# A new order of pieces in a fused attention and feed-forward kernel: chunk 0 projected block by block, logits in one group of eighty matmuls, softmax subtraction in place

## The chip, the cores and the metric

The kernel runs on one core of a Trainium2 chip. The metric is device time in microseconds (us) of one execution; three runs of the kernel before gave 234.38, 235.88 and 237.16 us, so its median is 235.88 us. Five engines work side by side: TensorE (PE in the profile; its weight loads are PEld), VectorE (DVE), ScalarE (ACT), GpSimd (POOL) and SyncE (SP), which here only issues DMAs. Each engine runs its own instructions strictly in the order in which the program lists them, and waits at one when an input or a buffer isn't ready.

## The reference

x is 2048 x 640 in bfloat16. The reference normalises it and adds two branches to it:

```python
xn = _layernorm(x, axis=-1)
return x + _A_ref(xn, A_wqkv, A_wo) + _B_ref(xn, B_w1, B_b1, B_w2, B_b2)

# A: attention of each position to 8 positions, 2 apart, back from itself; 32 heads of 20
qkv = (x @ wqkv) ...                       # 640 -> 3 * 640
idx = pos[:, None] - (jnp.arange(8) * 2)[None, :]
logits = jnp.einsum("bhsd,bhswd->bhsw", q, kg) * scale      # masked where idx < 0
o = jnp.einsum("bhsw,bhswd->bhsd", _softmax(logits), vg)
return o @ wo
# B: feed-forward, 640 -> 1536 -> 640
h = _gelu(x @ w1 + b1)
return h @ w2 + b2
```

## The kernel before, in words

The 2048 rows are cut in four chunks of 512 (CH), and each chunk in four blocks of 128. Channels lie on partitions in five tiles of 128 (KT). For each chunk n the work is:

- **Normalise and turn.** bn_stats on DVE (`do_st`, L437, two halves a block), sqrt on ACT (L458), reciprocal on DVE (L462). In chunk 0, DVE writes the normalised block (L478), PE turns it by five transposes (`do_tp`, L493) into PSUM, and ACT or DVE copies it to xnT (`do_tc`, L498). In chunks 1 to 3, ACT writes the normalised block xn (L474) and a DMA transpose on SP's queue turns it (`do_td`, L505). xn has two buffers, so ACT's third block of a chunk waits until the first block's DMA transpose has landed.
- **Projections.** q, k, v = xnT x wqkv. In chunks 1 to 3: fifteen pieces `pj` of five 128x512 matmuls (L537), each copied from PSUM by ACT (`pc`, L596). In chunk 0 before: q of blocks 0 and 1 in 128-column pieces (L550), everything else for pairs of blocks in 256-column pieces (L581).
- **Logits.** DVE multiplies q with k at each of the 8 offsets (`qk`, L611, eight instructions). PE sums over a head with twenty matmuls for each pair of offsets (L633). `do_max` (L646) and `do_sub` (L653) on DVE, exp on ACT (L663), sums, reciprocal and division on DVE (L669 to L681). DMAs spread the result over the 20 channels of a head (`ax<-attn`, L691: half on SP's queue, half on ACT's).
- **Values.** DVE multiplies v with ax (`av`, L707, eight), adds (L716, three) and writes oT (`ot`, L722).
- **Feed-forward.** PE: twelve pieces `f1` a chunk (L729, five 128x512 matmuls each); ACT: gelu (L740).
- **Output.** For each block five pieces `o`: four over the feed-forward's h, the fifth over oT (L760 for 512 columns, L762 for the other 128, seventeen pairs of matmuls in all). ACT copies it (L767, L768) and POOL adds it to the output with an accumulating DMA (L773). Before that, x is copied to the output by a plain DMA on SP's queue (`xp`, L514), and the bias b2 is added by an accumulating DMA that POOL issues (`xb`, L518) once that copy has landed.

Matmul results of the projections, `f1` and chunk 0 share four PSUM buffers ("acc"). The products `qk` and `av` share four SBUF buffers ("prod"). The logits have one PSUM tile.

**What sets the order.** `make_plan` (L149) lists all pieces with an engine, an estimated duration, a rank, the pieces they need and their buffers. `Plan.run` (L57) lays them out in time by these estimates: on each engine the ready piece with the lowest rank goes next. The program is emitted in that order. The table `RANK` shifts the rank of whole groups of pieces. So a changed rank, estimate or due time reorders the instructions of PE, DVE, ACT and SP, and nothing reorders them on the chip.

**Names used below**: `pj`, `f1`, `o`, `lg` (logits matmuls), `qk`, `av`, `ot`, `xn` and `tc` as above, then the chunk, then block or piece; `xd` and `xs` are the spreading DMAs on SP and ACT, `ld` is the loading of w2, wo and b2.

**In the emitted order of before** SP issues, after the first loads: the four transposes of chunk 1, `ld`, the four copies `xp0` to `xp3`, `xd0`, the eight transposes of chunks 2 and 3, `xd1` to `xd3`. POOL issues `xb0` to `xb3` as the copies land. PE has, around the middle of the span: eight `f1` of chunk 1, then the `pj` of chunk 2. ACT has, between the copies of chunk 1's and chunk 0's projections and the first gelu of chunk 1: `xn22` and `xn23`.

Of the kernel before, what the change touches and what calls it, by code (L numbers as in the profile page):

```python
# [10 lines left out]
ACT = mybir.ActivationFunctionType  # L11
# [7 lines left out]
class Plan:  # L19
# [112 lines left out]
RD = float(D) ** -0.5  # L132
# [3 lines left out]
WARM = 40  # L136

COLS = ((0, 2), (2, 4), (4, 5))
# [4 lines left out]
    "ad02": 84.2, "av1": 114.8, "f11": 43.4, "f12": 139.3, "f13": 100, "gc4": -2.7, "hj0": 28.1, "hj2": 111.9,  # L143
    "o00": 7.2, "o03": 101.7, "o20": 120, "o31": 66.5, "ot2": 46.1, "pc11": -88.8, "pj31": 84.9, "pj32": 89.2,
    "qk0": -89.8, "qk2": 80.3, "st0": 12.4,
# [3 lines left out]
def make_plan(fns, offsets=RANK):  # L149
# [11 lines left out]
    def turned(n, pair=None):  # L161
        if n:
            return [f"tc{n}{bl}" for bl in range(BPC)]
        every = ["tc00a", "tc00b", "tc01a", "tc01b", "tc02", "tc03"]
        return every if pair is None else every[4 * pair : 4 + 4 * pair]

    def done(n, which):
        if n:
            return [f"pc{n}{which}{to}" for to in range(KT)]
        return (["gc0", "gc1", "gc4"] if which == 0 else [f"hc{which}0{g}" for g in range(len(COLS))]) + [  # L170
            f"hc{which}1{g}" for g in range(len(COLS))
        ]

    pl.add("b1", VE, 0.1, -90, [], f("b1"), after=20.0)
    for n in range(NCH):
# [6 lines left out]
        for bl in range(BPC):  # L182
            land = (3.1, 3.6, 6.1, 8.7)[bl] if n == 0 else (0.0, 12.9, 21.8, 21.8)[n]
            r = -40 if n else -99
            if n == 0 and bl == 1:
                pl.add("sm", SE, 0.75, -99, [], f("sum1"), after=land)
                pl.add("nm", SE, 0.3, -99, ["sm"], f("neg1"))
                pl.add("me", VE, 0.12, -98, ["sm"], f("mean1"))
                pl.add("sq", SE, 0.75, -99, ["nm"], f("sq1"))
                pl.add("rs01", SE, 0.3, -99, ["sq"], f("sqrt", 0, 1, 2), table="sqrt")  # L190
                pl.add("rc01", VE, 0.16, -99, ["rs01", "me"], f("rstd", 0, 1, 2))
                continue
            pl.add(f"st{n}{bl}a", VE, 0.42, r, [], f("st", n, bl, 0), after=land)
            pl.add(f"st{n}{bl}", VE, 0.65, r, [f"st{n}{bl}a"], f("st", n, bl, 1), after=8.0 if n == 0 and bl == 2 else 0.0)
            if n == 0:
                pl.add(f"rs{n}{bl}", SE, 0.3, -100, [f"st{n}{bl}"], f("sqrt", n, bl, bl + 1), table="sqrt")
                pl.add(f"rc{n}{bl}", VE, 0.16, -99, [f"rs{n}{bl}"], f("rstd", n, bl, bl + 1))
# [3 lines left out]
        for bl in range(BPC):  # L201
            xn, tp = ("xn", n, bl), ("acc", "tp", n, bl)
            if n > 0:
                pl.add(f"xn{n}{bl}", SE, 0.81, early + -4.0, [f"rc{n}"], f("xn", n, bl), [xn])
                pl.add(f"tc{n}{bl}", DQ, 4.0 if n > 1 else 2.7, early - 3.0, [f"xn{n}{bl}"], f("td", n, bl), [xn, xnT], 22.0)
                continue

            if bl == 0:
                for u, a, b, eng, own in (("a", 0, 2, VE, "lo"), ("b", 2, KT, SE, "hi")):
                    us = (b - a) / KT  # L210
                    pl.add(f"xn00{u}", VE, 0.06 + 0.5 * us, -99, ["rc00"], f("xn", 0, 0, a, b), [xn])
                    pl.add(f"tp00{u}", PE, 0.54 * us, -99, [f"xn00{u}"], f("tp", 0, 0, a, b, own), [xn])
                    pl.add(f"tc00{u}", eng, 0.16 + 0.49 * us, -99, [f"tp00{u}"], f("tc", 0, 0, a, b, eng), [xnT])
                continue
            pl.add(f"xn0{bl}", VE, 0.42, -99, [f"rc0{bl}"], f("xn", 0, bl), [xn])
            pl.add(f"tp0{bl}", PE, 0.3, -99, [f"xn0{bl}"], f("tp", 0, bl, 0, KT), [xn, tp])
            for u, a, b, eng in (("a", 0, 2, VE), ("b", 2, KT, SE)) if bl == 1 else (("", 0, KT, SE),):
                pl.add(f"tc0{bl}{u}", eng, 0.16 + 0.49 * (b - a) / KT, -100 if bl == 1 else -99, [f"tp0{bl}"], f("tc", 0, bl, a, b, eng), [tp, xnT])
        if n == 1:
            pl.add("ld", DQ, 9.2, -1000, turned(1), f("ld"))  # L220
# [3 lines left out]
        if n == 0:  # L224
            wq, wk, wv = 5.4, 8.3, 11.1
            A, B, C = ("acc", "qa"), ("acc", "qb"), ("acc", "qc")
            pl.add("ga", PE, 0.056 * 10, -60, ["tc00a"], f("ga", 0, 2), [xnT, A, B], wq)
            pl.add("gb2", PE, 0.056 * 5, -60, ["tc00b", "ga"], f("ga", 2, 3), [xnT, A, B], wq)
            pl.add("gb3", PE, 0.056 * 5, -60, ["gb2"], f("ga", 3, 4), [xnT, A, B], wq)
            pl.add("gb4", PE, 0.056 * 5, -60, ["gb3"], f("ga", 4, KT), [xnT, A, B], wq)  # L230
            pl.add("gd", PE, 0.056 * 10, -59, ["tc01a", "gb4"], f("gd", 0, 2), [xnT, B, C], wq)
            pl.add("ge", PE, 0.056 * 15, -59, ["tc01b", "gd"], f("gd", 2, KT), [xnT, B, C], wq)
            pl.add("gc0", SE, 0.54, -50, ["gb4"], f("gc", 0), [A, q])
            pl.add("gc1", SE, 0.54, -50, ["ge"], f("gc", 1), [C, q])
            pl.add("gc4", SE, 0.3, -50, ["ge"], f("gc", 4), [B, q])
            for which, buf, land in ((0, q, wq), (1, k, wk), (2, v, wv)):
                for pair in range(0 if which else 1, 2):
                    for g, (a, b) in enumerate(COLS):
                        ps = ("acc", "gp", which, pair, g)
                        nm = pl.add(f"hj{which}{pair}{g}", PE, 0.55 * (b - a), -50 + which // 2, turned(0, pair), f("gp", which, pair, a, b), [xnT, ps], land)  # L240
                        pl.add(f"hc{which}{pair}{g}", SE, 0.3 * (b - a), -50, [nm], f("gq", which, pair, a, b), [ps, buf])
        for which, buf in enumerate((q, k, v)):
            for to in range(KT if n else 0):
                ps = ("acc", "p", n, which, to)
                r = early + (0 if which < 2 else 20.0)
                pl.add(f"pj{n}{which}{to}", PE, 1.08, r, turned(n), f("pj", n, which, to), [xnT, ps])
                pl.add(f"pc{n}{which}{to}", SE, 0.52, early + 0.0, [f"pj{n}{which}{to}"], f("pc", n, which, to), [ps, buf])
# [6 lines left out]
        for wp in range(W // 2):  # L254
# [4 lines left out]
            group = 2 if n else 4  # L259
            if wp % group == group - 1:  # L260
                wps = range(wp - group + 1, wp + 1)
                need = [f"qk{n}{x}{i}" for x in wps for i in range(2)] + ([f"lg{n}{wp-group}"] if wp > group else [])
                every = [("prod", "qk", n, x) for x in wps]
                pl.add(f"lg{n}{wp}", PE, 0.16 + 0.52 * group, n - 1000, need, f("lg", n, wps), every + [L], slack=0.8)

        e, at, ax = ("e", n), ("attn", n), ("ax", n)
        m, rs, ss, z = ("m", n), ("rs", n), ("ss", n), ("prod", "z", n)
# [3 lines left out]
        pl.add(f"mx{n}", VE, 1.22, n - 1000, [f"m{n}"], f("sub", n), [L, m, z])  # L271
        pl.add(f"ex{n}", SE, 1.02, n - 1000, [f"mx{n}"], f("exp", n), [z, e], table="exp")
# [16 lines left out]
        for ft in range(FT):  # L289
            ps = ("acc", "h", n, ft)  # L290
            pl.add(f"f1{n}{ft}", PE, 1.08, base + 10.0 + 1.0 * ft, turned(n), f("f1", n, ft), [xnT, ps], 15.8 if ft < FT // 2 else 18.5)
# [25 lines left out]
def kernel(  # L317
# [50 lines left out]
    w1_v = B_w1.rearrange("(t p) n -> p t n", p=P)  # L368

    def load_x(b0, b1):  # L370
        nc.sync.dma_start(x_sb[:, b0:b1, :], x_nb[:, b0:b1, :])  # L371

    def load_w(s, a=0, b=KT):
        nc.sync.dma_start(wqkv[s][:, a:b, :], wqkv_v[:, a:b, s * D : (s + 1) * D])  # L374

    load_x(0, 1)
    load_x(1, 2)
    load_w(0, 0, 2)
    load_w(0, 2, KT)
    load_x(2, 3)  # L380
    load_w(1)
    load_x(3, BPC)
    load_w(2)
    nc.sync.dma_start(b1_rt[0:FT, :], B_b1.rearrange("(t p) -> t p", p=P))
    load_x(BPC, 2 * BPC)
    for c in range(2):
        cs = slice(c * F // 2, (c + 1) * F // 2)
        nc.sync.dma_start(w1_sb[:, :, cs], w1_v[:, :, cs])
    nc.sync.dma_start_transpose(b1_t[:], b1_rt[:])
    load_x(2 * BPC, NCH * BPC)  # L390
# [7 lines left out]

    ident = consts.tile([P, P], BF16, name="ident")
# [4 lines left out]
    nc.scalar.activation(warm[:], nc.const_aps.tensor(0.0, [P, 1], F32), ACT.Sqrt)  # L404
# [16 lines left out]
    acc1 = consts.tile([P, 1], F32, name="acc1")  # L421
    neg1 = consts.tile([P, 1], F32, name="neg1")
# [17 lines left out]

    def trash():
        return get(("xn", 0, 1), lambda: lnp.tile([P, D], BF16, tag="xn", name="xn"))

    def do_sum1():
        nc.scalar.activation(trash()[:], x_sb[:, 1, :], ACT.Identity, accum_out=acc1[:])

    def do_neg1():
# [387 lines left out]
```

## Time and profile before

| what | value |
|---|---|
| runs | 234.38, 235.88, 237.16 us; median 235.88 |
| the profiled execution | 234.38 us; its span in the trace 232.2 us, so 2.2 us lie outside the span |
| PE | 209.6 us busy, 1564 matmuls |
| DVE | 174.8 us busy, 177 instructions |
| ACT | 112.4 us busy, 192 instructions |
| POOL | 19.7 us busy |
| matmul 128x512: busy, and start to start in a row | 379 ns; 0.216 us |
| `qk` or `av` (128x2560) | 1484, 1486 ns |
| add (128x5120) | 2823 ns |
| max, subtract, divide (128x1024) | 1223, 1224, 1225 ns |
| exp, f32 from SBUF; a load of an activation table | 1058 ns; 1283 ns |
| gelu, 128x512 from PSUM; copy of 128x512 from PSUM | 688; 583 to 587 ns |
| DMA transpose, issue to landing: least, median, most | 2.6, 3.4, 16.1 us |

Times are in us from the start of the span. A busy matmul row overlaps the next one, so a piece's price on PE is read from start to start, not from its busy time. In the list of waits a row is: who waited <- for what: total us, times, longest. In the timelines a row is: start, length, engine, line, operation, tiles, count, and in brackets the idle time before it and what ended it. "Start to start" of the groups used below: `f1` 1.08 us (60 matmuls in 12.95), `pj` 1.088 us (50 in 10.88), an `o` pair 0.2717 us (12 pairs in 3.26), 128-column projections 0.0606 us each (35 in 2.12), 256-column ones 0.109 us each (25 in 2.73), eighty logits matmuls 2.30 us, forty 1.21 us.

### The profile page before, as it was taken

To read this page: it belongs to the slowest core of one execution; us is meant where nothing else is said; L and a number is where in the kernel's file an instruction comes from. 1 tells how busy PE (TensorE), PEld (TensorE's weight loads), DVE (VectorE), ACT (ScalarE), POOL (GpSimd) and SP (SyncE) were. 2 spreads that over 40 slices of the span, in tenths; PEclk is the share of its full clock that TensorE was granted. 3 is DMA by queue.
4 is the path that set the end of the run, shared out by engine and by line. 5 is a ranking of instruction groups with operands and counts; after the bars stand their busy time and mean duration, and the time that the engine had idled before them with its cause. 6 is when DMAs were issued, how large, how long until landed. Compare 5 with 4: busy or idle time off the path is not lost.

```text
span 232.2 us, 3724 instructions
## 1 busy us (share of the span) xinstructions
PE 209.6 (90%) x1564; PEld 121.1 (52%) x1564; DVE 174.8 (75%) x177; ACT 112.4 (48%) x192; POOL 19.7 (8%) x37
## 2 busy tenths in 40 slices
PE   8789999999940999999999999999999999996960
PEld 7788447557510355655555555555455554553540
DVE  4456998969599980789998999999994607999100
ACT  6378976878004856572273845222633722610111
POOL 2000000080000000011010001111101110010111
PEclk9999999999995699999999999999999999999997
DMA  6999549999995212018220018222200292001322
GB/s 189 341 368 334 60 105 388 386 199 211 132 187 75 45 32 55 0 8 201 31 28 3 0 16 195 29 28 31 30 0 3 28 200 40 0 3 27 54 28 34
DMA packets 24152, 23.93 MB, mean 103 GB/s; under 512 B 9160, under 2 KB 21960, under 8 KB 24136
## 3 DMA queue, kind: packets, MB, share of 16 engines
q1 hardware_dynamic: 18696, 16.66, 27.4%
q0 software_dynamic: 4144, 4.92, 15.8%
q10 hardware_dynamic: 1296, 2.13, 3.2%
q8 instruction: 12, 0.20, 0.3%
q14 instruction: 4, 0.03, 0.0%
HBM read 10.00 MB, written 7.54 MB: 76 GB/s over the span
## 4 chain that ended last, share of the span: by engine, by line
PE 47%; issue 33%; DMA 10%; POOL 4%; ACT 2%; SPq 1%; DVE 1%; POOLq 0%
PE pps L537 21%; PE hps L729 11%; DMA xnT<-xn 7%; PE lo L760 6%; PE gps L581 5%; POOL out_dram L773 4%; DMA x_sb<-in_A_x_dram 3%; PE L L633 3%; PE hi L762 1%; ACT hT L740 1%; SPq L374 1%; SPq L371 1%; ACT L740 1%; DVE stats L437 0%; POOLq L830 0%
## 5 line engine op out<-in xcount | busy, mean ns | idle before, releaser
L729 PE MATMUL hps<-xnT,w_sb 128*128 128x512 bf16 x240 | 55.9, 387 | 9.7 <-ACT hT L740 9.7
L707 DVE TENSOR_TENSOR pv<-vT,ax 128x2560 bf16<-128x2560 bf16 x32 | 45.8, 1486 | 12.1 <-DMA ax<-attn 11.2
L760 PE MATMUL lo<-w_sb,hT 128*128 128x512 bf16 x192 | 53.4, 379 | 0.0
L611 DVE TENSOR_TENSOR prod<-qT,kT 128x2560 bf16<-128x2560 bf16 x32 | 45.5, 1484 | 1.0 <-ACT qT L591 0.9
L729 PEld LDWEIGHTS <-w_sb 128*128 128x128 bf16 x240 | 23.3, 99 | 37.7 <-issue 12.3
L762 PE MATMUL hi<-w_sb,hT 128*128 128x128 bf16 x192 | 40.2, 219 | 0.0
L740 ACT ACTIVATE hT<-hps,b1T 128x512 bf16<-128x512 f32 x48 | 31.6, 688 | 16.3 <-PE hps L729 11.8
L767 ACT CAST osb<-lo 128x512 bf16<-128x512 f32 x15 | 8.8, 587 | 56.3 <-PE hi L762 34.7
L716 DVE TENSOR_TENSOR pv<-pv 128x5120 bf16<-128x5120 bf16 x12 | 33.9, 2823 | 0.3
L760 PEld LDWEIGHTS <-hT 128*128 128x128 bf16 x192 | 18.7, 98 | 22.6 <-issue 0.4
L773 POOL DMA_DIRECT2D out_dram<-osb x15 | 12.9, 863 | 163.7 <-ACT osb L768 163.7
L760 PE MATMUL lo<-wo,oT 128*128 128x512 bf16 x80 | 23.0, 379 | 1.8 <-DVE oT L722 1.8
L762 PEld LDWEIGHTS <-hT 128*128 128x128 bf16 x192 | 18.3, 98 | 1.8 <-issue 0.2
L437 DVE BATCH_NORM_STATS2 stats<-x_sb 128x6 f32<-128x320 bf16 x30 | 13.0, 468 | 8.2 <-DMA x_sb<-in_A_x_dram 8.2
L474 ACT ACTIVATE xn<-x_sb,nmr,rstd 128x640 bf16<-128x640 bf16 x12 | 11.1, 923 | 14.0 <-DMA xnT<-xn 14.0
L537 PE MATMUL pps<-xnT,wq_sb 128*128 128x512 bf16 x75 | 17.1, 380 | 0.0
L762 PE MATMUL hi<-wo,oT 128*128 128x128 bf16 x80 | 16.9, 219 | 0.0
L537 PE MATMUL pps<-xnT,wk_sb 128*128 128x512 bf16 x75 | 16.7, 379 | 0.0
L537 PE MATMUL pps<-xnT,wv_sb 128*128 128x512 bf16 x75 | 16.7, 379 | 0.0
L760 PEld LDWEIGHTS <-oT 128*128 128x128 bf16 x80 | 7.8, 98 | 11.3 <-DVE oT L722 2.1
L537 PEld LDWEIGHTS <-wk_sb 128*128 128x128 bf16 x75 | 8.7, 118 | 7.4 <-issue 0.2
L537 PEld LDWEIGHTS <-wv_sb 128*128 128x128 bf16 x75 | 8.7, 118 | 7.4 <-issue 0.2
(72 smaller groups left out, 194.0 us busy)
## 6 DMA issues: line engine op xcount, KB each, us to landing
out_dram<-osb POOLq DMA_DIRECT2D x15, 160.0 KB, 3.3
ax<-attn SPq DMA_DIRECT2D x8, 256.0 KB, 6.5
ax<-attn ACTq DMA_DIRECT2D x8, 256.0 KB, 6.6
w_sb<-in_B_w_dram SPq DMA_DIRECT2D x2, 960.0 KB, 12.2
w_sb<-in_B_w_dram SPq DMA_DIRECT2D x1, 1920.0 KB, 8.2
out_dram<-x_sb SPq DMA_DIRECT2D x3, 640.0 KB, 12.5
out_dram<-b2bc POOLq DMA_DIRECT2D x3, 640.0 KB, 19.8
x_sb<-in_A_x_dram SPq DMA_DIRECT2D x1, 1280.0 KB, 9.7
```

The lines of the kernel that those rows point to most:

```text
L437: nc.vector.bn_stats(stats[:, i, :], x_sb[:, b, i * (D // 2) : (i + 1) * (D // 2)])
L474: nc.scalar.activation(xn[:], x_sb[:, i, :], ACT.Identity, bias=nmr[:, i : i + 1], scale=rstd[:, i : i + 1])
L537: nc.tensor.matmul(ps[:], lhsT=wqkv_p[which][:, ti, to, :], rhs=xnT[:, ti, :], start=(ti == 0), stop=(ti == KT - 1),)
L581: nc.tensor.matmul(ps[:, to - a, :], lhsT=wqkv_p[which][:, ti, to, :], rhs=tiles["xnT", 0][:, ti, pair * 2 * P : (pair + 1) * 2 * P], star ...
L611: nc.vector.tensor_tensor(out=prod[:, i, :, :], in0=qkv_tile(n, 0)[:], in1=qkv_tile(n, 1)[:, :, off : off + CH], op=ALU.mult,)
L707: nc.vector.tensor_tensor(out=pv[:, i, :, :].rearrange("p t (j c) -> p t j c", j=BPC), in0=qkv_tile(n, 2)[:, :, off : off + CH].rearrange( ...
L716: nc.vector.tensor_tensor(out=ta[:], in0=ta[:], in1=tb[:], op=ALU.add)
L729: nc.tensor.matmul(ps[:], lhsT=w1_sb[:, ti, ft * P : (ft + 1) * P], rhs=tiles["xnT", n][:, ti, :], start=(ti == 0), stop=(ti == KT - 1),)
L740: nc.scalar.activation(hT[:], tiles["hps", n, ft][:], ACT.Gelu_apprx_tanh, bias=b1T[:, ft : ft + 1], scale=1.0)
L760: nc.tensor.matmul(lo[:], lhsT=lhs, rhs=rhs[:, 0:CH], start=first, stop=last)
L762: nc.tensor.matmul(hi[:, 0 : D - CH], lhsT=lhs, rhs=rhs[:, CH:D], start=first, stop=last)
L773: nc.gpsimd.dma_start(rows, tiles["osb", n, bl][:], accum_op=ALU.add)
```

## The change

- **Loads.** Block 1 of x is issued from ACT's queue; wq comes in one transfer, not two; blocks 2 and 3 of x in one transfer behind wk; all of x before w1; w1 in one transfer, behind b1's transpose.
- **Chunk 0.** Block 1's mean and variance come from bn_stats as the others' do (no sums on ACT). The transposes use the "acc" buffers. q, k and v of chunk 0 are computed block by block in 128-column pieces (`gj`, copied by `gc`): for each block four groups of q, of k, the fifth tiles of q and k together, v, and v's fifth tile.
- **Warm-up.** 44 matmuls on a tile of zeros in place of 40 on ones.
- **Logits.** Every chunk's eighty logits matmuls follow one another and the first waits for all eight products. Before, chunks 1 to 3 did forty after the fourth product and forty after the eighth (chunk 0 all eighty at the end).
- **Softmax.** The subtraction writes back to PSUM and exp reads PSUM; before, it wrote an SBUF tile out of the four "prod" buffers.
- **Order.** `RANK` and some due times differ.

The emitted order of each engine changes with it. After the first loads SP now issues: the transposes of chunk 1, `ld`, `xp0`, the transposes of chunk 2's blocks 0 and 1, `xd0`, those of blocks 2 and 3, `xp1`, `xp2`, the transposes of chunk 3, `xd1`, `xp3`, `xd2`, `xd3`. PE's pieces after chunk 0's projections: `f100` to `f107`, `pj100` to `pj102`, `lg0`, the other twelve `pj` of chunk 1, eight `f1` of chunks 0 and 1 in turn, `lg1`, `f1011`, `f115`, `o000` to `o003`, fifteen `pj` of chunk 2, ten of chunk 3, `o004`, `f116`, `o010` to `o013`, `lg2`, ... ACT has `pc113`, `xn22`, `pc114`, `pad21`, `pc120`, `xs0`, `pc121`, `pc122`, `xn23`; later `ge15`, `ex1`, `xn32`, `pc210` to `pc213`, `xn33`. DVE has the statistics of chunk 2 ahead of the first `qk0`, those of chunk 3 behind the last, then the softmax of chunk 0, all eight `qk1`, `av000`, `av001`, the maximum of chunk 1 and so on.

```diff
-WARM = 40
-COLS = ((0, 2), (2, 4), (4, 5))
+WARM = 44
+GROUPS = (((0, 0, 4),), ((1, 0, 4),), ((0, 4, 5), (1, 4, 5)), ((2, 0, 4),), ((2, 4, 5),))
 RANK = {
-    "ad02": 84.2, "av1": 114.8, "f11": 43.4, "f12": 139.3, "f13": 100, "gc4": -2.7, "hj0": 28.1, "hj2": 111.9,
-    "o00": 7.2, "o03": 101.7, "o20": 120, "o31": 66.5, "ot2": 46.1, "pc11": -88.8, "pj31": 84.9, "pj32": 89.2,
-    "qk0": -89.8, "qk2": 80.3, "st0": 12.4,
+    "ad00": 18.6, "ad12": 90.3, "av1": 24.9, "f10": 124.1, "f11": 78.6, "f12": 77, "f13": 59.1, "gc3": 128,
+    "gj1": 27.5, "gj2": -11.5, "o00": -229.5, "o22": 117, "o31": 152.4, "ohi": 184, "ot0": -109.4, "pj21": -3.6,
+    "pj32": 101.5, "qk1": -201.6, "qk2": -177.8, "qk3": -48.2, "rs2": 121.5, "st2": 89.3, "st3": 723.2, "tc2": 50.7,
+    "tc3": 81.9, "xn0": -29.1,
 }
...
-    load_x(0, 1)
-    load_x(1, 2)
-    load_w(0, 0, 2)
-    load_w(0, 2, KT)
-    load_x(2, 3)
-    load_w(1)
-    load_x(3, BPC)
-    load_w(2)
+    nc.sync.dma_start(x_sb[:, 0, :], x_nb[:, 0, :])
+    nc.scalar.dma_start(x_sb[:, 1, :], x_nb[:, 1, :])
+    for s in range(3):
+        nc.sync.dma_start(wqkv[s][:], wqkv_v[:, :, s * D : (s + 1) * D])
+        if s == 1:
+            nc.sync.dma_start(x_sb[:, 2:BPC, :], x_nb[:, 2:BPC, :])
     nc.sync.dma_start(b1_rt[0:FT, :], B_b1.rearrange("(t p) -> t p", p=P))
-    load_x(BPC, 2 * BPC)
-    for c in range(2):
-        cs = slice(c * F // 2, (c + 1) * F // 2)
-        nc.sync.dma_start(w1_sb[:, :, cs], w1_v[:, :, cs])
+    for cs in (slice(BPC, 2 * BPC), slice(2 * BPC, NCH * BPC)):
+        nc.sync.dma_start(x_sb[:, cs, :], x_nb[:, cs, :])
     nc.sync.dma_start_transpose(b1_t[:], b1_rt[:])
-    load_x(2 * BPC, NCH * BPC)
+    nc.sync.dma_start(w1_sb[:], B_w1.rearrange("(t p) n -> p t n", p=P))
...
+    def do_gj(bl, g, a, b):
+        cs = slice(bl * P, (bl + 1) * P)
+        ps = get(("gps", bl, g), lambda: psA.tile([P, BPC, P], F32, tag="acc", name="gps"))
+        slots = [(which, to) for which, lo, hi in GROUPS[g] for to in range(lo, hi)]
+        pairs = [(i, ti) for i in range(len(slots)) for ti in range(a, b)]
...
+        for i, ti in pairs:
+            which, to = slots[i]
+            nc.tensor.matmul(
+                ps[:, i, :],
+                lhsT=wqkv_p[which][:, ti, to, :],
+                rhs=tiles["xnT", 0][:, ti, cs],
...
-            group = 2 if n else 4
-            if wp % group == group - 1:
...
+        need = [f"qk{n}{x}{i}" for x in range(W // 2) for i in range(2)]
+        for wp in range(W // 2):
+            us, slack = (0.5, 0.0) if wp else (0.74, 0.8)
+            need = [pl.add(f"lg{n}{wp}", PE, us, n - 1000, need, f("lg", n, wp), [("prod", "qk", n, wp), L], slack=slack)]
...
     def do_sub(n):
-        z = prodp.tile([P, W, P], F32, tag="prod", name="z")
-        tiles["z", n] = z
+        L = tiles["L", n]
         nc.vector.tensor_tensor(
-            out=z[:],
-            in0=tiles["L", n][:],
+            out=L[:],
+            in0=L[:],
...
-        nc.scalar.activation(e[:], tiles["z", n][:], ACT.Exp, scale=SCALE)
+        nc.scalar.activation(e[:], tiles["L", n][:], ACT.Exp, scale=SCALE)
...
-        ones = nc.const_aps.tensor(1.0, [P, P], BF16)
-            nc.tensor.matmul(idle[:, 0, :], lhsT=ones, rhs=ones, start=True, stop=True)
+            nc.tensor.matmul(idle[:, 0, :], lhsT=zeros[:], rhs=zeros[:], start=True, stop=True)
```

## The prediction, before the result was known

> **What bounds the kernel now.** I read the busy shares first: PE 90%, DVE 75%, ACT 48%. So PE sets the pace, and the question is where it stands idle. The stretches of the span answer that.
>
> ```profile
> PE 209.6 (90%) x1564; PEld 121.1 (52%) x1564; DVE 174.8 (75%) x177; ACT 112.4 (48%) x192; POOL 19.7 (8%) x37
> ```
>
> ```profile
> 12.60:66.40 53.80, 53.73 (x424) 34.47 (x425) 43.82 (x72) 36.74 (x62) 5.33 (x4) 1.00 0.99 238
> 66.40:76.00 9.60, 0.02 (x1) 0.02 (x1) 9.56 (x6) 3.88 (x5) 0.00 (x0) 0.64 0.76 118
> 76.00:212.90 136.90, 136.90 (x954) 72.52 (x953) 112.93 (x79) 63.17 (x105) 10.36 (x12) 0.99 0.24 43
> 212.90:214.70 1.80, 0.00 (x0) 0.00 (x0) 1.65 (x2) 0.00 (x0) 0.00 (x0) 1.00 0.01 5
> 214.70:232.20 17.50, 9.54 (x76) 5.59 (x76) 0.98 (x2) 2.26 (x6) 2.58 (x3) 0.93 0.26 38
> ```
>
> Columns: stretch, length, then busy us of PE, PEld, DVE, ACT and POOL, granted clock, share of the DMA engines. From 12.6 to 212.9 PE has one hole, 66.4 to 76.0, and then a short one. The waits say what ended each.
>
> ```profile
> ACT xn L474 <- DMA xnT<-xn: 14.0, 2, 11.1
> ...
> DVE pv L707 <- DMA ax<-attn: 11.2, 3, 8.2
> DVE m L646 <- PE L L633: 9.9, 2, 8.1
> PE hps L729 <- ACT hT L740: 9.7, 1, 9.7
> ...
> PE lo L760 <- DVE oT L722: 1.8, 1, 1.8
> ```
>
> ACT shows the first link: a normalised block waits for a transposed one, and the gelus behind it wait too.
>
> ```profile
> 57.88 0.25 ACT L603 COPY vT<-vT 128x70 bf16<-128x70 bf16 x1
> 69.19 0.92 ACT L474 ACTIVATE xn<-x_sb,nmr,rstd 128x640 bf16<-128x640 bf16 x1 [11.06 <-DMA xnT<-xn]
> 73.01 0.92 ACT L474 ACTIVATE xn<-x_sb,nmr,rstd 128x640 bf16<-128x640 bf16 x1 [2.90 <-DMA xnT<-xn]
> 73.95 1.28 ACT L740 ACT_TABLE_LOAD   x1
> 75.24 1.84 ACT L740 ACTIVATE hT<-hps,b1T 128x512 bf16<-128x512 f32 x3
> ```
>
> ```profile
> 75.98 6.15 PE L729 MATMUL hps<-xnT,w_sb 128*128 128x512 bf16 x20 [9.65 <-ACT hT L740]
> ```
>
> So xn22 stood from 58.1 to 69.2 for a transpose that SP issued at 53.5; PE filled the four accumulators with f1 pieces and then stood 9.65 us. The usual landing is 3.4 us after issue, this one took 15.7: the DMA engines were 99% busy from 12.6 to 66.4, and POOL's four accumulating bias DMAs, issued from 46.1, lay across it. The hole costs more than itself: twenty f1 matmuls took 6.15 us afterwards and 4.48 before it, 1.67 more, with a granted clock of 0.64 in the hole.
>
> **The change, part by part.**
>
> *Start.* PE's first work in bulk waits for wk. In before it came at 10.46 with 160 KB of x ahead of it that now stand behind; at the 341 GB/s of that slice this is 0.47 us, so wk is here at 10.0. But PE now has the fifth tiles and k of block 0 ahead of q of block 1, so it has done only 20 of the 300 128-column matmuls by then. The other 280 at 0.0606 and two transposing groups at 0.27 give 10.0 + 17.0 + 0.5 = 27.5 for the first f1. Before, f1 began at 21.35 with 40 matmuls of 0.109 still owed, the same as 25.7. Cost 1.8. Bounds: 1.0 (wk half a microsecond sooner, a group in the gap) and 4.0 (x or a copy late: xn03 now stands on DVE behind the first statistics of chunk 1, whose data came at 15.3, and reaches PE at 17.0, 0.8 before PE asks for it). Four more warm-up matmuls at 0.10 and zeros for ones end before the first transposes matter: they are covered by the wait for wk. Block 1's statistics leave ACT (736, 186, 186, 828, 187 ns) and return to DVE as 0.9 + 0.2: also before 10.0. x of block 1 on ACT's queue: 0.4 of issue, covered likewise. w1 is one transfer behind all x: x chunk 1 came at 15.3; 1280 and 1920 KB more at 368 GB/s end at 24.0, before 27.5. If this cover went, f1 would wait the difference.
>
> [...] PE kept clock 1.00 through the 1.8 us hole and lost it in the 9.65 one. [...]
>
> *DVE's start.* The statistics of chunk 2 stand ahead of qk0 now: DVE has them done at 25.1 (from 15.3: 1.1 for the begun block, 0.6 for xn03, seven more blocks at 1.0, small ones). k of the last block is copied at 25.6. So qk0 starts at 25.6, not 22.1. Eight at 1.42 end at 36.95, and PE, between f1 and pj pieces, has the logits at 42.2; maximum, subtraction, exp with its table (2.35 from the subtraction to the sums in before), sums, reciprocal, division: attn at 51.2, not 46.9. From there DVE runs all eight qk1 (62.6).
>
> *The hole.* xn20 and xn21 are now ahead: SP issues their transposes after one copy of x, not after four and xd0. `ld` and xp0 were 11.5 us from issue to xp0's end (33.98 to 45.44 with what stood before it); shifted by the start they end at about 48, and the transposes follow in the same queue at 49 to 52, beside one bias DMA, not four. ACT reaches xn22 at 49.9: it waits 0 to 2 us, and PE has four accumulators (4.3 us) in hand. The second pair, xn32 and xn33, are asked for at about 72 and 78; tc30 and tc31, issued at 65 and 70, share the DMA engines with two bias DMAs (1.28 MB at the 160 KB/us that POOL's queue reached at best: 8 us) and land by about 74 and 77; PE again has 4.3 us in hand. So I let the hole go: -9.65 and -1.67. Bounds 0 and -11.3. What is late next is DVE, see below.
>
> [...]
>
> *The end.* PE waited 1.81 us for the last oT at 212.9. DVE's work after ot2 is 8 av, 3 adds, ot: 11.4 + 8.5 + 1.5 = 21.4. By the walk below ot2 ends near 173 and ot3 near 195, while PE asks at 202. -1.8 (bounds 0, -1.8). The order of the last copies is as it was, so the tail after the last matmul, 224.2 to 232.2, stays at 8.0.
>
> *DVE against PE in the middle.* The logits of a chunk wait for all eight products, and av000 then waits for lg's first group, since the eight products hold all four prod buffers. Walking both by the order given: PE has lg0 done at 42.2, then 12 pj (13.1), 8 f1 (8.6), lg1 (2.3), 2 f1, 12 pairs of o (5.4), 25 pj (27.2): it asks for ot0 at 98.8. DVE starts av000 at 64.5, then 8 av (11.4), maximum and subtraction (2.4), sums to attn (3.75), 4 qk2 (5.7), 3 adds (8.5), ot (1.45): 97.7. PE then has 68 pairs of o (18.5), 13 f1 (14.0), 5 pj (5.4), lg2 (2.3) up to o104: 139.0. DVE has 4 qk2, waits for lg2's first group at 105.2, and the same 33.2 with 1.0 of waiting for exp: 139.4. In the same way o204 is asked for at 173.2 and ot2 ends at 173.3. They are level. Each handover to exp took 2.45 to 3.85 us in before, and I used 2.35 four times, with cover in three. So whatever DVE loses PE pays: I add 2.0 (bounds 0 and 6: three handovers at 1.4 too little, and 2 for a late ax or xn22).
>
> *Logits and softmax.* Eighty in a row are 2.30, twice forty 2.42: -0.12 for three chunks, -0.4. The subtraction into PSUM: mask's PSUM-to-PSUM row (0.288 for 128 elements) and 1.224 for 1024 from PSUM to SBUF lie on one line, 1.05 ns an element: the same 1.22; ends 1.1 and 1.4. exp from PSUM: copies of 128 and 512 from PSUM took 272 and 587 ns, which for 1024 gives 1.01; gelu's 688 doubled gives 1.38 as the upper end; I take 1.05, no change. All ends together, four chunks on DVE's path: -0.7 to +2.0, inside the 0 to 6 above. Three of ACT's twelve table loads go (1.28 each): ACT is 48% busy, no price.
>
> **Sum**, against the profiled execution's span of 232.2: +1.8 - 11.3 - 1.8 + 2.0 - 0.4 = 222.5. With 2.2 us outside the span, 224.7 against 234.4. The median of the runs is 1.5 above that execution: **226.2 us, about 4% faster**. Own range: 222.5 + (-0.8 - 2.0 - 0.5) = 219.2 to 222.5 + (2.2 + 4.0) = 228.7 in the span, 223 to 232.4 as a median.
>
> **Rivals.**
> 1. *The hole stays in another place.* One of the two pairs of transposes meets the bias DMAs as tc20 did. For: both pairs still stand in SP's queue next to copies whose landing releases bias DMAs; the waits of 11.1 and 2.9. Against: one or two bias DMAs, not four. Back come 9.65 + 1.67: span 233.8, median 237.5, within 1%.
> 2. *Slower: transposes starve at both places.* If each lands about 16 us after issue, as tc20 did, tc20 issued at 41 lands at 57 and holds pc114, and with it qk1, for 7 us; tc30 and tc31 then hold pc210 and pc213 until 82 and 88, 8 to 9 us more for PE, and each hole adds some 1.7 of half clock. 222.5 + 7 + 8.5 + 3.4 = 241.4, median 245. It decides from a landing of about 8 us: below, the accumulators cover it.
> 3. *DVE sets the pace.* All handovers at 3.85, ax late as in before (13.5 us from attn to the first av): +6 for +2, span 226.5, median 230.2. For: three level meetings. Against: each shift of PE gives DVE room again. Still faster.
> 4. *The hole is not worth its length*, since DVE, 2.1 us ahead of before at ot0, would have stood instead: half of it stays, 228, median 232. Against: DVE's idle rows of 8.1 and 8.2 us show room.
>
> **How the numbers follow.** Forecast (with 3 and 4, which end in or at its range) 0.73; rival 1, 0.14; rival 2, 0.13. The time is the likeliest, 226.2. The range reaches from 223 to 238, which leaves out rival 2 and some of the tails. A change under 1% (233.5 to 238.2) can't be told from none here. Faster 0.73, same 0.14, slower 0.13.
>
> **What would show it.** In the changed profile: first f1 at about 27.5 (over 29: the start was mis-sized); wk ending PE's wait at about 10.0; no PE idle time over 2 us between 28 and the end, and "ACT xn <- DMA xnT" under 4 us in all (else rival 1 or 2, and the clock row falls to 0.5 behind it); PE's waits for oT at most 2 us at three places (more: rival 3); subtraction 1.22 and exp 1.0 to 1.1 us. The forecast is wrong if PE's idle time beyond 28 exceeds 8 us.

## The result, and the profile after

The changed kernel took 218.87 us (median of 4 runs, 218.09 to 220.46) beside 235.13 us for the kernel before (4 runs): a ratio of 0.9348, interval 0.9246 to 0.945. That is 6.5% faster. The ratio compares the means of the fast runs (219.07 and 234.35 us): the slowest execution of before, 237.16 us, counts as slow and is left out. The prediction had said 4% and 226.2 us, with a range from 223; the time lies 4 us below that range. The profiled execution took 218.53 us, with a span of 216.4 us against 232.2 before and 222.5 in the sum.

First the busy shares of the kernel after, then the first two stretches as before and the rest up to 199.0 (columns again: stretch, length, busy us of PE, PEld, DVE, ACT, POOL, granted clock, DMA share).

```profile
PE 207.1 (96%) x1693; PEld 121.5 (56%) x1693; DVE 174.4 (81%) x178; ACT 107.0 (49%) x191; POOL 19.7 (9%) x37
```

```profile
12.60:66.40 53.80, 53.80 (x563) 34.67 (x561) 46.53 (x76) 43.02 (x76) 4.01 (x3) 1.00 0.85 218
66.40:76.00 9.60, 9.60 (x54) 5.33 (x53) 9.46 (x10) 7.12 (x11) 0.00 (x0) 1.00 1.01 143
76.00:199.00 123.00, 122.98 (x865) 66.07 (x863) 111.67 (x74) 49.19 (x88) 11.62 (x13) 1.00 0.29 52
```

PE's work is nearly the same amount, in a shorter span. The stretch from 66.4 to 76.0, in which PE had 0.02 us of work before, is now full although there is no less DMA traffic in it (1.01 against 0.76 in the last column but one; that column adds up the time of packets, so it can pass 1), and the clock stays at 1.00. The short hole for the last oT is gone too. PE has no idle time over 0.3 us between 9.23 and its last matmul at 209.82. What still waits is DVE and ACT:

```profile
DVE pv L628 <- PE L L555: 5.2, 3, 2.2
...
ACT osb L688 <- DMA out_dram<-osb: 3.7, 1, 3.7
...
ACT xn L419 <- DMA xnT<-xn: 2.5, 2, 2.1
...
DVE sums L590 <- ACT e L584: 2.1, 1, 2.1
```

The line of xn was 14.0 us before. The first line is new, and it is the opposite of what the sum had paid for: DVE waits for PE at the logits of three chunks, and PE, once its first work in bulk has begun, waits for DVE only some 0.2 us (at the third oT, see the part on the prediction).

### The profile page after: what moved, and what is told of

Its sections match the earlier page's. It is cut to its first block, busy times and chain, and to the rows that moved or that the text cites. A ratio compares the mean times of both kernels' runs of the same rounds, so it can differ in the third digit from the quotient of the medians.

```text
span 216.4 us, 3973 instructions
## 1 busy us (share of the span) xinstructions
PE 207.1 (96%) x1693; PEld 121.5 (56%) x1693; DVE 174.4 (81%) x178; ACT 107.0 (49%) x191; POOL 19.7 (9%) x37
## 4 chain that ended last, share of the span: by engine, by line
PE 60%; issue 30%; POOL 4%; DMA 3%; POOLq 0%; SPq 0%
PE pps L483 23%; PE hps L650 16%; PE lo L681 9%; PE gps L500 7%; POOL out_dram L694 4%; DMA wk_sb<-in_A_wqkv_dram 3%; PE L L555 3%; PE hi L683 2%; POOLq L750 0%; PE tp L436 0%; SPq L343 0%; SPq L340 0%; POOLq L694 0%
## 5 line engine op out<-in xcount | busy, mean ns | idle before, releaser
L650 PE MATMUL hps<-xnT,w_sb 128*128 128x512 bf16 x240 | 54.7, 379 | 0.0
L650 PEld LDWEIGHTS <-w_sb 128*128 128x128 bf16 x240 | 22.8, 98 | 26.4 <-issue 0.2
L688 ACT CAST osb<-lo 128x512 bf16<-128x512 f32 x15 | 8.8, 586 | 55.8 <-issue 25.7
L397 DVE BATCH_NORM_STATS2 stats<-x_sb 128x6 f32<-128x320 bf16 x32 | 13.9, 467 | 5.8 <-DMA x_sb<-in_A_x_dram 5.8
L483 PEld LDWEIGHTS <-wq_sb 128*128 128x128 bf16 x75 | 8.7, 117 | 7.4 <-issue 0.2
```

Source lines behind the costliest of these rows:

```text
L397: nc.vector.bn_stats(stats[:, i, :], x_sb[:, b, i * (D // 2) : (i + 1) * (D // 2)])
L483: nc.tensor.matmul(ps[:], lhsT=wqkv_p[which][:, ti, to, :], rhs=xnT[:, ti, :], start=(ti == 0), stop=(ti == KT - 1),)
L650: nc.tensor.matmul(ps[:], lhsT=w1_sb[:, ti, ft * P : (ft + 1) * P], rhs=tiles["xnT", n][:, ti, :], start=(ti == 0), stop=(ti == KT - 1),)
L688: nc.scalar.copy(osb[:, 0:CH], tiles["lo", n, bl][:])
```

## The experiments

Each is one edit to the kernel named. The pieces of the plan are moved in the emitted list by a helper:

```python
order = moved(make_plan(fns).run(), pieces, "after", anchor)
```

### What made the hole (three runs)

The theory: the four accumulating bias DMAs, released by x's copies, stretch the transpose tc20 until ACT, and behind it PE, stands. The rival: the many DMAs in general, or a piece order in which PE would have stood anyway.

**e1_copies_late**, to the kernel before: the transposes of chunk 2 ahead of three of the four copies.

```diff
-for t in make_plan(fns).run():
+order = moved(order, ["xp1","xb1","xp2","xb2","xp3","xb3"], "after", "tc23")
+for t in order:
```

> The kernel before, with the plain copies of x to the output of chunks 1 to 3 (and so POOL's bias additions, which follow them) moved behind the transposes of chunk 2; nothing else. Theory (POOL's accumulating bias DMAs starve the transposes): tc20 lands within 6 us of its issue instead of 15.7, ACT waits under 4 us at xn22 and xn23 instead of 14.0, PE's hole of 9.65 us and the 1.67 us of half clock go; the span falls from 232.2 to 221 to 224, the median to 224 to 227. Rival (the hole comes from where xn22 stands among ACT's copies, or from the copies and the spreading of attn): a hole of 7 us or more stays, span 229 to 234.

Ratio 0.9792 (0.9678 to 0.9905), median 229.42 us; the profiled execution, the fastest of the four, has a span of 224.5 against 232.2. The transpose tc20 landed 7.1 us after its issue in place of 15.7 (the expectation had said within 6). The hole of 9.65 is gone, and the clock was not halved before the end. PE's waits in this kernel:

```profile
PE pps L544 <- ACT qT L603: 2.4, 2, 1.6
PE lo L767 <- DVE oT L729: 1.7, 1, 1.7
...
PE pps L544 <- ACT kT L603: 0.6, 1, 0.6
```

So this one part of the change gives back a large part of the 11.3 us that hole and half clock had cost: 7.7 us by the two profiled executions, 4.9 by the ratio of the timed runs, whose median stayed above the expected 224 to 227. About 3 us turn into small waits between 75 and 83, since the moved bias DMAs now meet the transposes of chunk 3: the slowest landing of a transpose, from the tile's view, is

```profile
DMA to landing us min/median/max: 2.6/4.5/11.1
```

**e2_no_bias**, to the kernel before: b2 is not added to the output; copies, loads and spreading DMAs stay where they are.

```diff
-nc.gpsimd.dma_start(dst, b2bc[:]..., accum_op=ALU.add)
+pass
```

> The kernel before with the four accumulating DMAs that add b2 to the output left out (the output lacks b2 but for the last block); the copies of x stay where they were. Theory: the accumulating DMAs alone stretch the transposes, so the hole goes as in the run with late copies: span 220 to 224. Rival (plain copies and the spreading DMAs are traffic enough): tc20 lands 10 us or more after issue and a hole of 5 us or more stays, span 227 to 233.

Ratio 0.958 (0.9443 to 0.9716), that is 9.8 us. The profiled execution has a span of 223.9, as expected. Its landings, and the stretch in which before had its hole:

```profile
DMA to landing us min/median/max: 2.6/2.6/4.3
```

```profile
66.40:76.00 9.60, 9.55 (x43) 4.62 (x43) 9.57 (x6) 6.64 (x11) 0.00 (x0) 1.00 0.17 34
```

No transpose takes over 4.3 us, and no hole is left. (The clock was halved later, from 205.2 to 208.7, behind a wait of PE of 1.98 us for the last oT; the last section comes back to it.) The copies and the spreads are still issued, but without the bias DMAs beside them the spreads have landed by 54.5 (60.4 before), and tc20, issued at 55.0, lands 2.6 us later. So the bias DMAs made the hole, partly by holding up the spreads and partly by themselves: in before tc20 landed at 69.2, 8.8 us after the spreads. With four of them in flight tc20 took 15.7 us, with one (e1) 7.1, with none 2.6; but in the first two the spreads were in flight as well, and in the third they had landed, so these are not prices of a bias DMA alone. What a bias DMA does to a transpose inside the DMA engines, no run shows.

**e3_copies_early**, to the kernel after: the three copies, and so their bias DMAs, back behind the first one, ahead of all four transposes of chunk 2 (tc20 to tc23).

```diff
+order = moved(order, ["xp1","xb1","xp2","xb2","xp3","xb3"], "after", "xb0")
```

> The changed kernel, with its copies of x of chunks 1 to 3 (and so the bias additions) put right behind chunk 0's, ahead of the transposes of chunk 2, as in the kernel before; nothing else. Theory: tc20 and tc21 lie behind three more copies and beside four bias DMAs, land 10 us or more after issue, hold xn22 and xn23 on ACT; PE gets a hole of 6 to 12 us around 52 to 65 and a stretch of half clock, span from 216.4 to 224 to 230. Rival (the gain lies in chunk 0, the logits or the softmax): span stays within 216 to 219.

Ratio 0.958 (0.9465 to 0.9694), span 221.1, 4.7 more than the kernel after. The stall comes back, in its landings, in ACT and in PE. The tile's view, then ACT's waits, then the timeline:

```profile
DMA to landing us min/median/max: 2.6/3.6/17.2
```

```profile
ACT xn L426 <- DMA xnT<-xn: 8.8, 4, 4.6
```

```profile
50.87 0.92 ACT L426 ACTIVATE xn<-x_sb,nmr,rstd 128x640 bf16<-128x640 bf16 x1 [3.65 <-DMA xnT<-xn]
...
52.31 2.32 PE L490 MATMUL pps<-xnT,wv_sb 128*128 128x512 bf16 x9 [1.39 <-ACT kT L526]
...
55.96 1.24 PE L657 MATMUL hps<-xnT,w_sb 128*128 128x512 bf16 x5 [1.33 <-ACT vT L526]
```

To read: ACT stands 3.65 us for a transpose, PE 1.39 and 1.33 us for ACT's copies behind it; later ACT stands 4.6 us for tc22, which took 17.2 us to land, and PE another 1.1. The direction is the theory's; the size is below its 224 to 230, and the clock was not halved. That the new order of PE's pieces did it alone, wherever the copies stand, is refuted by the 4.7 us. The rest of the 11.3 us does not come back. The new order gives ACT and PE other work between the late transposes and their first use, which would account for it; no run here takes that part of the order apart, so this is argued and not shown.

### How much room DVE has (two runs)

The sum held DVE and PE to be level and paid 2.0 us for it. Here DVE gets extra work ahead of the logits of chunk 1: the first product is formed three or five times (its value is the same).

```diff
+for _ in range(3 if (n, wp, i) == (1, 0, 0) else 1):   # e9: 5
     nc.vector.tensor_tensor(out=prod[:, i, :, :], ...)
```

> The changed kernel with the first product of chunk 1 computed three times over (two DVE instructions of 1.42 us more, 2.84 us). Theory (DVE and PE are level, but the logits of chunk 1 stand 1.4 us behind the last product on PE): PE waits about 1.4 us at the logits of chunk 1, then both are shifted alike; span 216.4 + 1.5 = 217.9 (217.2 to 218.4). Rival A (DVE has room): 216.4, no change. Rival B (every microsecond that DVE loses PE pays): 219.2 or more.

**e7_dve_plus_2p8** took 219.1 us, ratio 0.938 (0.9302 to 0.9459), span 217.0, which can't be told from the kernel after (its four spans reach from 216.0 to 218.3). So rival A holds. Of the 0.6 us between 217.0 and 216.4, PE's wait of 0.49 us at 74.14 is for a copy by ACT, and another execution of the unchanged kernel has one there too (0.22). At their turn at 61.40 the eighty logits matmuls show no wait, and DVE waits less for the logits than the 5.2 us of after:

```profile
48.67 14.35 DVE L535 TENSOR_TENSOR prod<-qT,kT 128x2560 bf16<-128x2560 bf16 x10
...
61.40 2.41 PE L556 MATMUL L<-prod,head_of 128*32 128x256 bf16 x80
```

```profile
DVE pv L629 <- PE L L556: 2.9, 2, 1.6
```

PE began at 61.40, while DVE was still forming products until 63.02. That can't be if the first logits matmul waits for all eight products. It doesn't: that is a need of the planner; on the chip each group of twenty waits for its own two products, and only the last group, at 61.40 + 3 x 0.575 = 63.1, needs the last product. In the kernel after the products end at 60.01 and the last group starts at 61.43 + 1.73 = 63.16, so the room for PE there is 3.1 us. DVE itself can lose 2.2 us there before its later work moves: that long it stood in after, at 62.21, for the logits to free a prod buffer. e7 bears this out: its oT came 0.66 us later than in after (96.11 for 95.45), which is 2.84 less 2.2, and PE used it at 96.80 without a wait.

> The kernel after with the first product of chunk 1 formed five times in place of once, some 5.7 us more of VectorE work ahead of the logits of chunk 1; the value is the same. Theory: TensorE's own work leaves VectorE about 3.1 us of room there, since each group of twenty logits matmuls waits for its own products alone; so about 2.5 us come through: span about 219, a TensorE wait for VectorE of 2 to 3 us at the logits of chunk 1 or right behind them. Rival: the room is larger than the run with 2.8 us could show, and nothing comes through: span 216.2 to 217.2. Second rival: VectorE has no room and all comes through: span about 222.

**e9_dve_plus_5p7** took 223.68 us, ratio 0.9491 (0.9387 to 0.9594), span 221.8. The span alone speaks for the second rival (no room, 222). The timeline says otherwise:

```profile
48.20 17.41 DVE L535 TENSOR_TENSOR prod<-qT,kT 128x2560 bf16<-128x2560 bf16 x12
```

```profile
60.92 1.27 PE L556 MATMUL L<-prod,head_of 128*32 128x256 bf16 x40
62.86 0.73 PE L556 MATMUL L<-prod,head_of 128*32 128x256 bf16 x20 [0.66 <-DVE prod L535]
65.66 1.26 PE L556 MATMUL L<-prod,head_of 128*32 128x256 bf16 x20 [2.07 <-DVE prod L535]
```

Forty matmuls run at once, then twenty wait 0.66 and the last twenty 2.07 us, each for its own products: 2.73 in all, where 5.68 less the room of 3.1 gives 2.6. The rest is the clock. The same stretch in windows of 1 us (the columns as before; the clock is the third number from the end):

```profile
64.00:65.00 1.00, 0.00 (x0) 0.00 (x0) 1.00 (x2) 0.00 (x0) 0.85 (x1) 0.94 1.18 200
65.00:66.00 1.00, 0.34 (x8) 0.31 (x11) 1.00 (x2) 0.00 (x0) 0.00 (x0) 0.50 1.20 189
...
71.00:72.00 1.00, 1.00 (x6) 0.51 (x5) 1.00 (x1) 0.66 (x1) 0.00 (x0) 0.65 0.31 61
```

The clock is halved from 64.9 to 71.7, and from 65.66 on PE works in it: 6.0 us at half speed are 3.0 us lost. 2.73 + 3.0 = 5.7, which is what the way from the first f1 to the last matmul grew by (190.3 against 184.6 in the run of after on this chip; 184.4 in the first profile of after, 184.5 to 185.3 in e4 to e7). So the theory's wait is right, and its span of 219 was wrong because it left the clock out.

### The grouping and the place of the subtraction (two runs)

**e4_two_groups**, to the kernel after: twice forty logits matmuls in chunks 1 to 3, as in before.

```diff
+order = moved(order, ["lg10","lg11"], "after", "f111")
+order = moved(order, ["lg20","lg21"], "before", "o004")
+order = moved(order, ["lg30","lg31"], "before", "o104")
```

> The changed kernel with the logits of chunks 1 to 3 again in two groups of forty: the first forty moved up on PE to where the first four products of the chunk are done. Theory (PE never waits for the logits or for DVE after them, so grouping only sets its own price): PE pays 0.12 us for each of three chunks, DVE's 5.2 us of waiting for the logits before the first values product shrink and are worth nothing; span 216.4 to 217.2. Rival (the single group is a part of the gain, since each change of PE to the logits costs more than its row shows): 218 or more. Second rival (DVE's waits of 5.2 us are on the path): under 215.5.

Ratio 0.9322 (0.9265 to 0.9379), span 216.9: no difference. DVE's 5.2 us of waits for the logits ahead of the values products are gone, but 3.8 us of waits for the logits stand ahead of the maximum in their place, and neither costs anything:

```profile
DVE m L575 <- PE L L562: 3.8, 3, 1.8
```

**e5_z_in_sbuf**, to the kernel after: the subtraction writes to SBUF again and exp reads it there.

```diff
-out=L[:], in0=L[:],
+out=z[:], in0=tiles["L", n][:],
```

> The changed kernel with the subtraction written to SBUF again (a tile out of the four prod buffers) and exp reading it there. Theory (in place is worth nothing): subtraction 1.224 us for 1.232, exp 1.058 for 1.024, four times, off PE; span 216.0 to 217.0. Rival (the fifth user of four buffers delays the values products): span 218 or more.

Ratio 0.9335 (0.9243 to 0.9427), span 216.1: no difference. The groups of after, then of this run (busy us in all, mean ns of one):

```profile
L574 DVE TENSOR_TENSOR L<-L,m 128x1024 f32<-128x1024 f32 x4 | 4.9, 1232 | 0.1
...
L584 ACT ACTIVATE e<-L 128x1024 bf16<-128x1024 f32 x4 | 4.1, 1024 | 1.8 <-DVE L L574 1.7
```

```profile
L575 DVE TENSOR_TENSOR z<-L,m 128x1024 f32<-128x1024 f32 x4 | 4.9, 1225 | 0.1
...
L585 ACT ACTIVATE e<-z 128x1024 bf16<-128x1024 f32 x4 | 4.2, 1058 | 1.8 <-DVE z L575 1.7
```

In place costs 7 ns on DVE and saves 34 ns on ACT, four times each. Neither this nor the grouping carries any gain that can be seen, which leaves the order of the pieces and the start; what the start gave is read from the trace below.

### The end (three runs)

From the last matmul to the end of the span before took 7.99 us, after 6.57. The prediction had 8.0 for both.

**e6_old_tail**, to the kernel after: the output pieces `o312` and `o313` ahead of `o304`, as in before.

```diff
+order = moved(order, ["o312","o313"], "before", "o304")
```

> The changed kernel with two output pieces (o312, o313: 1.63 us of PE) moved back ahead of o304, as in the kernel before, so that the last blocks' copies and output DMAs end 1.6 us later against the last matmul. Theory (the tail is a chain of two accumulating output DMAs on POOL, each some 3.3 us, that starts at o324's end): last matmul at 209.8 as before, end 8.0 us behind it instead of 6.5, span 217.9. Rival (the tail is set by the last matmul): span 216.4.

Span 217.6 with the last matmul at 209.64, so 7.98 from there to the end; ratio 0.9405 (0.9302 to 0.9508). In the median the 1.4 us are inside the interval, in the trace they are plain. The chain can be read in the tail of after:

```profile
210.39 0.59 ACT L688 CAST osb<-lo 128x512 bf16<-128x512 f32 x1 [3.72 <-DMA out_dram<-osb]
...
211.44 0.86 POOL L694 DMA_DIRECT2D out_dram<-osb  x1 [3.62 <-ACT osb L689]
```

and in that of before:

```profile
226.26 0.59 ACT L767 CAST osb<-lo 128x512 bf16<-128x512 f32 x1 [3.54 <-DMA out_dram<-osb]
...
227.31 0.86 POOL L773 DMA_DIRECT2D out_dram<-osb  x1 [3.44 <-ACT osb L768]
```

The last copy waits 3.5 to 3.7 us for an osb buffer, that is for the landing of the accumulating output DMA before it, and then an accumulating DMA of its own follows. In before this last DMA is issued 3.07 us behind the last matmul (which ends at 224.24), in after 1.62 us behind it (209.82). `o312` and `o313`, 1.6 us of PE's work, now lie behind the pieces that feed this chain and no longer ahead of them. So I tried what that points to.

**e8_last_block_last**, to the kernel after: the output pieces of the very last block (chunk 3, block 3) behind those of all other blocks, right ahead of the last step `ohi`. DVE, not ACT, copies this block, and it goes out by plain DMAs, without POOL.

```diff
+order = moved(order, ["o330","o331","o332","o333","o334","oclo"], "before", "ohi")
```

> The changed kernel with the pieces of the very last block (whose output goes out by plain DMAs without POOL) put behind those of all other blocks, 3.7 us of PE. Theory (the same chain): the accumulating DMAs start 3.7 us earlier against the last matmul, the end lies 2.5 to 4 us behind the last matmul; span 212.5 to 214. Rival (the last matmul sets the tail): 216.4.

216.47 us, ratio 0.9217 (0.9161 to 0.9274); the last matmul to the end is 2.80 us, as expected; the span, 214.7, is 0.7 above what was expected. Since a run's start differs by up to 2 us (wk came between 8.4 and 10.4 in the kernels built on after), I ran it again beside the kernel after on one chip.

> The changed kernel unchanged, for a time on the same chip as its neighbours here: 218 to 220 us, a ratio of 0.93 to 0.94 to the kernel before.

> The kernel after with its last block's output pieces put right ahead of the output's last step, once more, beside the kernel after on the same chip. Theory: the last matmul to the end falls from 6.6 us to about 2.8, and some of it is paid back by pieces that no longer stand between the others: 2 to 3.5 us less than the kernel after, whose span was 216.4. Rival: the first look was a draw of the start, and the two agree within 1 us.

The kernel after: 219.39 us (218.71 to 219.61), span 216.6, ratio 0.9317 (0.9244 to 0.9391). With the last block last: 216.28 us (215.66 to 217.11), span 214.3, ratio 0.9192 (0.9116 to 0.9269). The slowest run of the one is 1.6 us below the fastest of the other; the medians are 3.1 apart. The tail of the second run:

```profile
209.46 0.86 POOL L701 DMA_DIRECT2D out_dram<-osb  x1 [3.61 <-ACT osb L696]
...
211.56 0.29 DVE L718 TENSOR_TENSOR osb<-hi,x_sb 128x128 bf16<-128x128 f32 x1 [0.20 <-PE hi L690]
211.88 0.36 ACTq L721 DMA_DIRECT2D out_dram<-osb  x1
```

POOL's last accumulating DMA is issued 2.06 us ahead of the last matmul (211.52) and no longer 1.62 behind it, and the span ends with the plain DMA. PE pays a part of the 3.8 us back: its way from the first f1 to the last matmul grew by 1.5 us in this run (186.1 against 184.6) and by some 0.9 in the first (185.4). 0.7 of it is a wait for the same chain of buffers, which both runs show:

```profile
PE lo L688 <- ACT osb L695: 0.7, 1, 0.7
```

The other wait, 0.9 us at 74.45 for a copy by ACT, is not the edit's: the first run of it has none there, and executions of the kernel after have 0 and 0.22.

It beats both kernels.

## Why the prediction was right in direction and too small in size

- **The hole (-9.65 and -1.67): right.** ACT's wait for transposes fell from 14.0 to 2.5 us, under the 4 that the prediction set; the clock stays at 1.00. e1 and e2 show the cause from the side of before, e3 from the side of after. Rivals 1 and 2 did not come: the slowest transpose (tc20) landed 9.7 us after its issue, beyond the 8 us from which rival 2 was to decide, yet ACT began xn22 0.4 us behind that landing without standing for it, and PE never stood. Rival 4 did not come either: no part of the hole stayed. One reading on the way was wrong: 0.99 is not "99% busy", since that column adds up packet times; in tenths the page of before has 9 in most slices up to 66 us, but 5 and 4 between 23 and 35. Nothing hangs on it, for around tc20's 15.7 us it has 9.
- **The last oT (-1.8): right.** The last oT is ready at 195.47 and PE uses it at 198.67; this is read from the trace, and no run undoes it alone. The three meetings before it are as close as the prediction had them: oT is ready at 95.45, 135.82 and 170.51, and PE uses it at 96.14, 136.56 and 170.57. At the third PE does stand a little: that matmul starts 0.40 us behind the one before it and not 0.22, so some 0.2 us.
- **The start (+1.8): failed.** The first f1 came at 25.45, not at 27.5; against the 25.7 that before amounts to, this is -0.25. The step that failed is "the other 280 at 0.0606". That price came from dividing the length of a merged row of matmuls by their number, and the length includes the end of the last one, which runs on after the next has started. (The table ahead of the prediction calls it "start to start", which it isn't.) Start to start they take 0.0558 us (50 in 2.79, from 22.66 to the first f1): in the start of after, 20 of them take 1.28 us in a merged row, but the next group follows 1.11 us later.

```profile
10.94 1.28 PE L500 MATMUL gps<-xnT,wq_sb 128*128 128x128 bf16 x20
12.05 1.28 PE L500 MATMUL gps<-xnT,wk_sb 128*128 128x128 bf16 x20
```

  Over 280 matmuls this is 1.3 us. The other 0.8 is wk, at 9.23 and not 10.0. The clock took nothing in the start: from 4.50 to 10.00, where PE was busy for 3.76 of the 5.50 us, it was at 1.00.
- **DVE against PE (+2.0): failed.** The walk that found the two level was right (above). The step that failed is "So whatever DVE loses PE pays: I add 2.0". What it paid for did not come: DVE stood for exp once, 2.1 us in chunk 0, and never for ax (11.2 us before); PE paid about 0.2. Nor does PE pay for what DVE loses ahead of the logits: e7's 2.84 us cost nothing that can be told from the spread, since DVE had stood there for PE, and e9 shows PE's own room, 3.1 us, because each twenty wait for their own pair. "The logits of a chunk wait for all eight products" is only the planner's need (the section on the change tells it that way too); in the walk it cost nothing, as by its figures PE came to lg1 at 63.9 (42.2 + 13.1 + 8.6), behind the last product at 62.6. Rival 3 did not come. What DVE would lose between the logits and oT no run tests; at the third meeting there is no room for it.
- **The end ("the tail after the last matmul stays at 8.0"): failed by 1.4 us.** I took the order of the last copies to fix it, and not what PE still does behind the piece that feeds the last copy. e6 puts the 1.4 us back.
- **Logits and softmax (-0.4): too small to be seen.** The prices came as said (the eighty 2.3 us, the subtraction 1.23, exp 1.02); e4 and e5 undo them without a difference.

The sum with the measured terms, and the -0.4 as predicted: 232.2 - 0.25 - 11.3 - 1.8 + 0.2 - 0.4 - 1.4 = 217.25, against 216.4; 0.85 us are not accounted for. Of the 7.3 us between 226.2 and 218.87, 6.1 lie in the span, and 1.2 in the step from one execution to the median: the profiled execution of before lay 1.5 us below its median, that of after 0.3. Three terms erred on the same side: the start by 2.05 us, DVE against PE by 1.8, the end by 1.4. The lower end of the range took the start at +1.0 and DVE at 0, and left the end at 8.0; the start went 1.25 below its bound.

## What to carry to other kernels

Before paying for a meeting of two engines, look for what the instruction on the chip waits for: a planner's needs can be coarser than the semaphores, and here the last product could come 3.1 us later than it did before PE stood for it; and ask whether the other engine is not the one that stands there already. Take the rate of a row of short matmuls from start to start, never from a merged length. And read the tail as a chain of its own: what counts is how long before the last matmul its first link can begin, and moving a block that does not feed it behind those that do gave a further 3 us.

## What the runs showed of the hardware

- The time of a DMA transpose from issue to landing differed with what else was in flight. tc20 took 2.6 us when copies and spreads had landed and there were no bias DMAs (e2), 7.1 beside one accumulating bias DMA and the last of the spreads (e1), 15.7 beside the spreads and four bias DMAs (before). A long one came without a bias DMA too: in the kernel after tc20, issued at 36.80 with the loads of w2 and wo and a copy of x in flight and no bias DMA yet, took 9.7. There it cost PE nothing: ACT had other work until 46.91, and the landing was at 46.52.
- A halved clock followed even short waits of PE. Two of 0.66 and 2.07 us with 0.73 us of work between them were followed by it (e9, from 64.9 on, within the second), and in e2 one single wait of 1.98 us was:

```profile
204.65 0.39 PE L760 MATMUL lo<-wo,oT 128*128 128x512 bf16 x1 [1.98 <-DVE oT L722]
...
206.22 0.63 PE L760 MATMUL lo<-wo,oT 128*128 128x512 bf16 x1
```

  The same matmul takes 0.63 us there for 0.38. The 1.81 us of before, the 1.7 of e1, and 1.39 and 1.33 us with 2.3 us of work between them (e3) were not followed by it. The half clock began 2.6 us (e2), 2.7 (e9) and 2.8 (the hole of before) after PE first stood idle, and lasted about 3.5, 6.8 and 10.2 us. No wait of PE beside it was longer than 2.07 us in e2 and e9. What sets these waits apart from those that it did not follow, no run shows.
